# Fused attention, experts and dense layer: all weights through one ring of eight buffers, float64 pieces converted in place

## The chip, the cores and the metric

The kernel runs on one core of one Trainium2 chip. The metric is the device time of one execution in microseconds (us); lower is better. TensorE (PE) multiplies matrices, VectorE (DVE) and ScalarE (ACT) work on tiles in on-chip memory, GpSimd (POOL) and SyncE (SP) issue most of the DMA transfers here, and 16 DMA engines move the data.

## The reference

Three layers in a row on 1152 tokens: attention in a window of 64 positions, a mixture of eight experts of which each token goes to one, and a dense layer whose two weight matrices arrive as float64.

```
q, k, v: (2, 8, 576, 64) f32;   N, D, E, F = 1152, 512, 8, 1024
x = softmax(q k^T / 8, window of 64) v          -> (1152, 512)

expert_idx = argmax(x @ w_gate)                 # each expert takes at most 288 tokens
y = relu(x_e @ w1[e]) @ w2[e];  x = gate * y    # w1 (8,512,1024), w2 (8,1024,512) f32

h = x @ w_in                                    # w_in (512, 2048) float64
g = h * clip(h + 3, 0, 6) / 6
out = (g @ w_out).astype(float32)               # w_out (2048, 512) float64
```

## The kernel before

**Stages.** Attention and routing take the first 67 us or so. Then come 32 expert units and eight dense units. A unit is a quarter of an expert's weights (256 of 1024 inner columns) or an eighth of the dense layer's (256 of 2048): two halves, h = 0 for the up product and h = 1 for the down product, each 128 x 1024 float32 words. Expert units are called m0 to m31 here, dense units d0 to d7. They are worked off in three teams of experts and then in four groups of tokens of the dense layer:

```
ORDER = ('awwbawbwawbwabww', 'awwawwawwaww', 'awwbawbwaabwbwww')
GROUPS = [(0, 640, 0, NDS // 2), (640, 512, 0, NDS), (0, 384, NDS // 2, NDS), (384, 256, NDS // 2, NDS)]
```

A letter is one step of PE: `w` is half a unit of the team's large expert (208 to 256 tokens), `a` a unit of a smaller one, `b` a unit of a second small one, which in two teams is "tiny" (64 tokens). m0 to m11 belong to the first team; m2, the first `b`, is tiny. A dense step f uses unit f // 2: group 0 (640 tokens) takes d0 to d3 with eight steps, group 1 (512 tokens) all eight units. A step of the dense layer is called up(f) and down(f); PE does up(0), up(1), down(0), up(2), down(1) and so on.

**Weights.** Every product is made of three passes of rounded operands: hi x hi, lo x hi, hi x lo. So each loaded half is split in two pieces by `split_ops`: ACT casts hi (L263), and DVE subtracts for lo (L268), into one of eight `wt` buffers. Only a tiny unit is used by PE as loaded, and holds its `raw` buffers until then. Float64 has no hardware type: a "piece" is 128 x 512 float64 words, read as 128 x 1024 32-bit words, and `conv64` makes float32 of it in six steps: ACT abs (L207) and round (L210), DVE clamp (L214), shift (L218), join (L223) and add (L232). Four pieces are a dense unit.

**Buffers and queues.** `rawp` has six buffers of 4 KB in each partition for expert halves and for converted dense halves; `cv` has three `raw64` buffers of the same size for float64 pieces, and two of 2 KB each for `c64` and `t64`. SP issues the expert loads (L276, L279) and the float64 pieces of d2 to d7. GpSimd issues the gathers of tokens (L801), the eight pieces of d0 and d1 (L198, L201), which are converted while the experts run, stored to DRAM from `t64` (L235, `wd_dram`) and loaded again as float32 halves (L1130) ahead of the dense layer.

**Order.** The instructions of an engine run in the order in which the program writes them. A planner in the kernel's Python code makes this order: `add_job` gives each load, conversion and split a due time in units, and `advance` puts the first job in due order that fits into the estimated gaps of an engine. The ring objects (`r_raw`, `r_64`, `r_t`, `r_wt`) hold a job back until the planner's estimate has a buffer for it. In the dense layer each block of PE (`d_stage`) is followed by ACT r (L1554), DVE gf (L1557), ACT hi (L1560) and DVE g (L1563). The token matrix of the dense layer is x2, written by ACT and DVE at the end of each expert (L1384, L1386).

Of the kernel before, what the change touches and what calls it, by code (L numbers as in the profile page):

```python
# [9 lines left out]
F32 = mybir.dt.float32  # L10
# [13 lines left out]
def tile_kernel(ctx, tc, q, k, v, w_gate, w1, w2, w_in, w_out, out, cap):  # L24
# [152 lines left out]
    HW = UW // 4  # L177
    NSC = 2
    cv = ctx.enter_context(tc.tile_pool(name="cv", bufs=2))
    wd_dram = [dram.tile([128, UW], F32, name=f"wd_dram{u}") for u in range(NSC)]  # L180
    w_in32 = w_in.bitcast(U32)
# [3 lines left out]

    def conv64(u, i, dst):

        box = {}  # L190

        queue = nc.gpsimd if u < NSC else nc.sync

        def load():
            box["raw"] = raw = cv.tile([128, 2 * HW], U32, name="raw64", bufs=NR64)
            if i < 2:
                src = w_in32[256 * i : 256 * i + 256, 2 * FU * u : 2 * FU * u + 2 * FU]
                queue.dma_start(raw.rearrange("p (c f) -> p c f", c=2), src.rearrange("(c p) f -> p c f", p=128))  # L198
            else:
                r0 = FU * u + 128 * (i - 2)  # L200
                queue.dma_start(raw, w_out32[r0 : r0 + 128, :])  # L201
            w = raw.rearrange("p (n t) -> p n t", t=2)
            box["lo"], box["hi"] = w[:, :, 0], w[:, :, 1]

        def c_abs():
            box["c"] = cv.tile([128, HW], U32, name="c64", bufs=NC64)
            nc.scalar.activation(box["c"].bitcast(F32), box["hi"].bitcast(F32), AF.Abs)  # L207
# [29 lines left out]
        return load, c_abs, c_round, c_clamp, c_shift, a_join, t_add, store  # L237

    NR64, NC64, NT64 = 3, 2, 2

# [82 lines left out]
    with ExitStack() as actx:  # L323
# [482 lines left out]
        def early_gather(e):  # L806
            box["xE"] = t = cv.tile([128, HW], U32, name="c64", bufs=NC64).bitcast(F32)
            rows_of(t, eI[:, 1:2], 128 * NE)
# [29 lines left out]
        def early_relu(u):  # L838
            def run(e):
                if "hfE" not in box:  # L840
                    box["hfE"] = cv.tile([128, HW], F32, name="t64", bufs=NT64)
                    box["hE"] = cv.tile([128, HW], F32, name="t64", bufs=NT64)
# [29 lines left out]
        def early_out(e):  # L872
            box["yE"] = t = cv.tile([128, HW], U32, name="c64", bufs=NC64).bitcast(F32)
            copy(e, t, box["aE"])
# [86 lines left out]
        def first_gather(e):  # L961
            box["x0"] = t = cv.tile([128, HW], U32, name="c64", bufs=NC64).bitcast(F32)
            rows_of(t, sidx[:, 3 * RANKS[0] : 3 * RANKS[0] + 1])
# [57 lines left out]
    NWT = 4  # L1021
    NRAW = 3
    NPC = 4
# [46 lines left out]
    AHEAD = (3.0, 1.5)  # L1070
    ZDUE = 3

# [23 lines left out]

    r_raw, r_wt, r_64, r_ct, r_t = Ring(2 * NRAW), Ring(2 * NWT), Ring(NR64), Ring(NC64), Ring(NT64)

# [4 lines left out]

    wt_at, raw_at = {}, {}
    for m in range(len(units)):
# [4 lines left out]
    raw_t, raw_ready, wt, half_ready, stored, pieces = {}, {}, {}, {}, {}, {}  # L1110
    e_of = {}
# [6 lines left out]
    def load_job(m, h):  # L1118
        kind, s, u = units[m]

        def gate():
            if kind == "d" and stored.get((u, h), 0) < 2:
                return None
            return r_raw.free(raw_at[m, h])

        def run(e, fin):
            take_raw(m, h)
            t = raw_t[m, h]
            if kind == "d":
                nc.gpsimd.dma_start(t, wd_dram[u][:, HALF * h : HALF * h + HALF])  # L1130
            else:
                if u == 0:
                    e_of[s] = expert(s)
                x = e_of[s]
                weights_in(t, x, u, h)
# [7 lines left out]
    def conv_job(u, i, m=None):  # L1143
        h = i // 2
        ix = {}

        def dst():
            return None if m is None else raw_t[m, h][:, HW * (i % 2) : HW * (i % 2) + HW]

        load, c_abs, c_round, *mid, t_add, store = conv64(u, i, dst)  # L1150

        def gate_load():
            a = 0.0 if m is None or (m, h) in raw_t else r_raw.free(raw_at[m, h])
            b = r_64.free()
            return None if a is None or b is None else max(a - 2.0, b)

        def run_load(e, fin):
            if m is not None and (m, h) not in raw_t:
                take_raw(m, h)
            ix["raw"] = r_64.take()  # L1160
            load()
            return (fin if m is not None else spend("D", 1.46, fin)) + 2.0

# [12 lines left out]
        def run_add(e, fin):  # L1176
            if m is None:
                ix["t"] = r_t.take()
            t_add()
            r_64.rel[ix["raw"]] = r_ct.rel[ix["ct"]] = fin  # L1180
            if m is not None:
                raw_ready[m, i] = fin + 0.2
            return fin + 0.2

        def run_store(e, fin):
            store()
            r_t.rel[ix["t"]] = fin + 5.0
            stored[u, h] = stored.get((u, h), 0) + 1
            return fin

        now = lambda: 0.0
        ops = [({"D": 1.46} if m is not None else {"P": 1.1}, gate_load, run_load), ({"A": 0.6}, r_ct.free, run_abs)]
        ops.append(({"A": 0.57}, now, plain(c_round)))
        ops += [({"V": c}, now, plain(fn)) for c, fn in zip((0.34, 0.34, 0.61), mid)]
        ops.append(({"V": 0.61}, now if m is not None else r_t.free, run_add))
        return ops + ([({"P": 1.1}, now, run_store)] if m is None else [])

    def split_job(m, i):
# [8 lines left out]
        def run_high(e, fin):  # L1207
            if (m, h) not in wt:
                r_wt.take()
                wt[m, h] = wp.tile([128, 2, HALF], F32R, name="wt")  # L1210
            n = HALF // 2
            r = raw_t[m, h][:, n * (i % 2) : n * (i % 2) + n]
            high, box["low"] = split_ops(wt[m, h], r, i % 2)
            high(e)
            return fin + 0.2

        def run_low(e, fin):
            box["low"]()
            pieces[m, h] = pieces.get((m, h), []) + [fin]
            if len(pieces[m, h]) == 2:  # L1220
                r_raw.rel[raw_at[m, h]] = half_ready[m, h] = max(pieces[m, h])
            return fin
# [444 lines left out]
    def dense_again():  # L1667

        for t0 in range(0, NTOK, 512):
            n = min(512, NTOK - t0)  # L1670
            acc = [bank("acc") for _ in range(n // 128)]
            for u in range(DFF // FU):
                halves = [wk.tile([128, 2, NC, 256], F32R, name="xT256", bufs=XTB) for _ in range(2)]
                halves = [x.rearrange("p a c f -> p a (c f)") for x in halves]
                for i in range(NPC):
                    r = wk.tile([128, HW], F32, name="xg", bufs=3)
                    if u < NSC:
                        nc.sync.dma_start(r, wd_dram[u][:, HW * i : HW * i + HW])
                    else:
                        load, *mid, t_add, _ = conv64(u, i, lambda: r)  # L1680
                        for fn in (load, *mid, t_add):
                            fn()
                    high, low = split_ops(halves[i // 2], r, i % 2)
# [188 lines left out]
    est["D"] = max(est["D"], done["rk"] + 1.7)  # L1872
    for ring, t in ((r_64, est["P"]), (r_ct, done["g0"] + 4.0), (r_t, done["g0"] + 4.0)):
        ring.rel = [t] * ring.n
# [113 lines left out]
```

## Time and profile before

| | |
|---|---|
| median of three runs | 435.39 us (435.08 to 438.6) |
| the profiled execution's own time | 434.86 us |
| its span, first to last instruction | 432.9 us |
| granted TensorE clock, mean | 0.992 |
| PE busy | 406.1 us, 94% |
| DVE busy | 290.0 us, 67% |
| ACT busy | 241.4 us, 56% |
| DMA, mean over the span | 171 GB/s, 73.89 MB |

Busy shares are means over stages that differ; the tables by window and the rows of single engines below are read by stage. Start times are counted from the first instruction of the span. A step "start to start" is the difference of the start times of two neighbours in a timeline, since the listed durations of neighbours overlap.

### The profile page before, as it was taken

The page shows a single profiled execution, that of the slowest core. Times are in us where ns is not written, and L with a number is a line of the kernel's source. Part 1 is how long each engine was busy: PE and PEld are TensorE (multiplying, and loading weights), DVE is VectorE, ACT ScalarE, POOL GpSimd, SP SyncE. Part 2 cuts the span into 40 slices and gives each one's busy share as a digit, 9 for nine tenths or more (in the row PEclk, how much of TensorE's full clock was granted, in tenths as well). Part 3 has the DMA queues.
Part 4 walks back from the last instruction along what each step waited for, and adds up shares of the span by engine and source line. Part 5 has one row for each costly group of instructions (what it writes and reads, how often), then busy time and mean ns, then how long its engine had stood idle before and what let it go on. Part 6 is the DMA issues. An engine that isn't in the chain of part 4 may idle for free.

```text
span 432.9 us, 8533 instructions
## 1 busy us (share of the span) xinstructions
PE 406.1 (94%) x3055; PEld 345.4 (80%) x3055; DVE 290.0 (67%) x800; ACT 241.4 (56%) x527; POOL 62.5 (14%) x128
## 2 busy tenths in 40 slices
PE   7999888798899999999999999999999999999991
PEld 4887664597778989987899898888888888899981
DVE  2888967687789999717579999989843222323430
ACT  4886773584569887526587766577543222322320
POOL 8633405025022001000200000000000000200210
PEclk9999999999999999999999999999999999999996
DMA  9997857989999999656924465543100000100101
GB/s 172 203 232 179 273 216 233 363 288 372 364 313 372 287 344 286 198 180 216 385 91 135 117 172 162 150 142 105 44 0 0 2 0 2 60 37 2 49 30 51
DMA packets 67762, 73.89 MB, mean 171 GB/s; under 512 B 31008, under 2 KB 49440, under 8 KB 67712
## 3 DMA queue, kind: packets, MB, share of 16 engines
q1 hardware_dynamic: 63760, 59.79, 46.6%
q0 software_dynamic: 3952, 13.47, 8.4%
q8 instruction: 26, 0.43, 0.4%
q14 instruction: 24, 0.20, 0.1%
HBM read 66.44 MB, written 6.82 MB: 169 GB/s over the span
## 4 chain that ended last, share of the span: by engine, by line
PE 65%; DVE 14%; DMA 10%; ACT 5%; issue 3%; POOL 0%; POOLq 0%; ACTq 0%; DVEq 0%; SPq 0%
PE banks L249 52%; DVE wt L268 4%; DMA raw<-in_moe_w_dram 4%; PE banks L506 2%; DMA c<-x_dram,eI 2%; PE banks L624 2%; DMA c<-x_dram,sidx 1%; PE banks L1493 1%; PE banks L1468 1%; PE banks L570 1%; PE banks L606 1%; DVE c L223 1%; DVE g L1563 1%; PE banks L663 1%; ACT wt L263 1%
## 5 line engine op out<-in xcount | busy, mean ns | idle before, releaser
L249 PE MATMUL banks<-x,wt 128*128 128x320 f32 (+3 forms) x576 | 107.4, 337 | 1.8 <-DVE wt L268 1.4
L249 PEld LDWEIGHTS banks<-x,wt 128*128 128x128 f32 x576 | 94.3, 188 | 12.2 <-DVE wt L268 2.2
L268 DVE TENSOR_TENSOR wt<-raw,wt 128x512 fp32r<-128x512 f32 x128 | 82.8, 684 | 14.9 <-ACT wt L263 14.3
L249 PE MATMUL banks<-wt,g 128*128 128x512 f32 x384 | 92.8, 390 | 0.0
L263 ACT CAST wt<-raw 128x512 fp32r<-128x512 f32 x128 | 74.6, 620 | 15.8 <-DMA raw<-in_moe_w_dram 9.4
L249 PEld LDWEIGHTS banks<-wt,g 128*128 128x128 f32 x384 | 71.6, 188 | 14.2
L1557 DVE SCALAR_TENSOR_TENSOR gf<-r,banks 128x320 f32<-128x320 f32 (+3 forms) x48 | 26.5, 552 | 54.5 <-ACT r L1554 54.3
L1554 ACT ACTIVATE r<-banks,c_three 128x320 f32<-128x320 f32 (+3 forms) x48 | 27.8, 579 | 58.3 <-PE banks L249 58.1
L249 PE MATMUL banks<-xT,wt 128*128 128x256 f32 (+2 forms) x288 | 39.0, 284 | 0.5 <-DVE wt L268 0.3
L249 PEld LDWEIGHTS banks<-xT,wt 128*128 128x128 f32 x288 | 35.1, 191 | 2.7 <-DVE wt L268 0.8
L249 PE MATMUL banks<-h,wt 128*128 128x256 f32 (+2 forms) x288 | 37.0, 279 | 0.0
L249 PEld LDWEIGHTS banks<-h,wt 128*128 128x128 f32 x288 | 34.6, 191 | 0.5 <-issue 0.5
L1563 DVE TENSOR_TENSOR g<-gf,g 128x320 fp32r<-128x320 f32 (+2 forms) x40 | 23.4, 584 | 12.3 <-ACT g L1560 11.6
L207 ACT ACTIVATE c<-raw 128x512 f32<-128x512 f32 x32 | 21.7, 677 | 17.1 <-DVE raw L232 6.3
L1560 ACT CAST g<-gf 128x320 fp32r<-128x320 f32 (+2 forms) x40 | 21.3, 533 | 16.3 <-DVE gf L1557 16.2
L1600 POOL DMA_INDIRECT out_dram<-raw,cidx x4 | 4.0, 992 | 163.8 <-ACT raw L1597 156.2
L249 PE MATMUL banks<-wt,xT 128*128 128x256 f32 x144 | 22.1, 294 | 3.0 <-DVE wt L268 2.2
L249 PEld LDWEIGHTS banks<-wt,xT 128*128 128x128 f32 x144 | 18.7, 190 | 5.7 <-DVE wt L268 3.6
L596 ACT ACTIVATE pe<-neg,nmx 128x128 f32<-128x128 f32 x72 | 22.3, 392 | 0.1
L583 DVE CUSTOM_DVE_ANT_0 neg<-banks,tmask 128x128 f32<-128x128 f32 x72 | 16.2, 285 | 9.1 <-PE banks L570 9.1
L223 DVE SCALAR_TENSOR_TENSOR c<-raw,c 128x512 uint32<-128x512 uint32 x32 | 22.0, 686 | 0.4
L210 ACT ACTIVATE raw<-raw 128x512 uint32<-128x512 uint32 x32 | 21.6, 674 | 0.0
(287 smaller groups left out, 556.0 us busy)
## 6 DMA issues: line engine op xcount, KB each, us to landing
raw<-in_moe_w_dram SPq DMA_DIRECT2D x64, 512.0 KB, 6.0
raw<-in_moe_w_in_dram SPq DMA_DIRECT2D x12, 512.0 KB, 3.8
raw<-in_moe_w_out_dram SPq DMA_DIRECT2D x12, 512.0 KB, 3.7
early<-in_moe_w_dram SPq DMA_DIRECT2D x8, 512.0 KB, 7.3
x_dram<-xt SPq DMA_DIRECT2D x9, 256.0 KB, 2.9
q_sb<-in_q_dram SPq DMA_DIRECT2D x8, 256.0 KB, 4.8
k_sb<-in_k_dram SPq DMA_DIRECT2D x8, 256.0 KB, 4.8
v_sb<-in_v_dram SPq DMA_DIRECT2D x8, 256.0 KB, 4.7
```

Of the source, the lines that this page charges most:

```text
L207: nc.scalar.activation(box["c"].bitcast(F32), box["hi"].bitcast(F32), AF.Abs)
L210: nc.scalar.activation(box["lo"], box["lo"], AF.Copy, scale=2.0 ** -29)
L223: nc.vector.scalar_tensor_tensor(out=box["c"], in0=box["hi"], scalar=0xC0000000, in1=box["c"], op0=ALU.bitwise_and, op1=ALU.bitwise_or,)
L249: nc.tensor.matmul(out, l, r, start=(start and n == 0), stop=(stop and n == len(pairs) - 1))
L263: nc.scalar.copy(hi, r)
L268: V.tensor_tensor(out=lo, in0=r, in1=hi.bitcast(F32), op=ALU.subtract)
L583: V.tensor_tensor_reduce(out=neg[:, hp, :], in0=box["sp", g][:, hp, :], in1=tmask[:, first, :], scale=-1.0, scalar=3.0e38, op0=ALU.add, op ...
L596: nc.scalar.activation(pe[:, hp, :], neg[:, hp, :], AF.Exp, bias=nmx[:, hp : hp + 1], scale=-1.0)
L1554: nc.scalar.activation(r, ph, AF.Relu, bias=c_three)
L1557: V.scalar_tensor_tensor(out=gf, in0=r, scalar=6.0, in1=ph, op0=ALU.min, op1=ALU.mult)
L1560: nc.scalar.copy(hi, gf)
L1563: V.tensor_tensor(out=lo, in0=gf, in1=hi.bitcast(F32), op=ALU.subtract)
```

## The change

One ring of `NRAW` = 8 buffers (the six and, in size, two of the three `raw64`) takes every load of weights, and its positions are fixed ahead: `raw_at` counts expert halves and float64 pieces in the order of units, with the pieces of d0 put behind the units `FIRST_AT` = 5, 9, 14 and 20. All of them are issued by SP. A float64 piece takes a whole buffer and is converted where it lies: the add writes over the low words, 8 bytes apart, and the split reads it there. Only d0 is converted among the experts, into four tiles of 2 KB (`first_w`) that stay on chip until the dense layer; nothing is stored to DRAM and loaded again. d1 is now treated like d2 to d7, with a due time of 1.5 units ahead of its own. `first_w` also serves the two tiles of the early expert that had used `t64`.

```diff
-    NRAW = 3
+    NRAW = 8
+    FIRST_AT = (5, 9, 14, 20)
...
-    rawp = ctx.enter_context(tc.tile_pool(name="rawp", bufs=2 * NRAW))
+    rawp = ctx.enter_context(tc.tile_pool(name="rawp", bufs=NRAW))
...
         def load():
-            box["raw"] = raw = cv.tile([128, 2 * HW], U32, name="raw64", bufs=NR64)
+            box["raw"] = raw = rawp.tile([128, 2 * HW], F32, name="raw").bitcast(U32)
...
-                queue.dma_start(raw, w_out32[r0 : r0 + 128, :])
+                nc.sync.dma_start(raw, w_out32[r0 : r0 + 128, :])
...
         def t_add():
-            d = dst()
-            if d is None:
-                box["t"] = d = cv.tile([128, HW], F32, name="t64", bufs=NT64)
-            nc.vector.tensor_tensor(out=d.bitcast(U32), in0=box["c"], in1=box["lo"], op=ALU.add)
-
-        def store():
-            nc.gpsimd.dma_start(wd_dram[u][:, HW * i : HW * i + HW], box["t"])
+            out = box["lo"] if dst is None else dst.bitcast(U32)
+            nc.vector.tensor_tensor(out=out, in0=box["c"], in1=box["lo"], op=ALU.add)
...
+    first_w = [cv.tile([128, HW], F32, name=f"first_w{i}", bufs=1) for i in range(4)]
...
     for m in range(len(units)):
+        if m != dense0:
+            for n in range(2 if units[m][0] == "e" else NPC):
+                raw_at[m, n] = len(raw_at)
+            for i in range(NPC):
+                if FIRST_AT[i] == m:
+                    raw_at[dense0, i] = len(raw_at)
         for h in range(2):
-            raw_at[m, h] = len(raw_at)
...
-            if kind == "d" and u >= NSC:
-                add_job(m - AHEAD[1] + 0.1 * i, m, conv_job(u, i, m))
+            if m == dense0:
+                add_job(FIRST_AT[i] + 1, FIRST_AT[i], conv_job(m, i))
             elif kind == "d":
-                add_job(m + ZDUE + 0.1 * i, m, conv_job(u, i))
-        if kind == "e" or u < NSC:
+                add_job(m - AHEAD[1] + 0.1 * i, m, conv_job(m, i))
+        if kind == "e":
```

PE's order of instructions is the same in both kernels. GpSimd's queue in the first expert team, the kernel before (`xg` is a gather of tokens, `raw64` a float64 piece, `t64` a converted one):

```order
L801 DMA xg_1512<-x_dram_78,sidx_130 64x512
L198 DMA raw64_1552<-in_moe2_w_in_dram 128x2x512
L198 DMA raw64_1554<-in_moe2_w_in_dram 128x2x512
L201 DMA raw64_1568<-in_moe2_w_out_dram 128x1024
L235 DMA wd_dram0_101<-t64_1666 128x512
L201 DMA raw64_1708<-in_moe2_w_out_dram 128x1024
L801 DMA xg_1785<-x_dram_78,sidx_130 128x512
L235 DMA wd_dram0_101<-t64_1781 128x512
L198 DMA raw64_1826<-in_moe2_w_in_dram 128x2x512
L801 DMA xg_1831<-x_dram_78,sidx_130 128x512
```

The same place on GpSimd's queue in the changed kernel:

```order
L791 DMA xg_1512<-x_dram_78,sidx_132 64x512
L791 DMA xg_1764<-x_dram_78,sidx_132 128x512
L791 DMA xg_1802<-x_dram_78,sidx_132 128x512
L791 DMA xg_1825<-x_dram_78,sidx_132 96x512
L791 DMA xg_2291<-x_dram_78,sidx_132 128x512
```

Only the gathers are left; the pieces of d0 stand in SP's queue, the first of them between the second half of m5 and the first half of m6.

DVE around the last writes of x2 ahead of the dense layer, the kernel before (`wt_3429` and `wt_3454` are the two halves of d0, `c64_3533` belongs to the first piece of d2):

```order
L268 TENSOR_TENSOR wt_3429<-raw_3347,wt_3429 128x512 x2
L1364 SCALAR_TENSOR_TENSOR h_3432<-banks_82,h_3432 128x208
L1344 TENSOR_LOAD offI_1458
L1412 ISA
L1412 TENSOR_TENSOR x2_1616<-banks_82,x2_1616 128x4x64
L268 TENSOR_TENSOR wt_3454<-raw_3349,wt_3454 128x512
...
L1386 TENSOR_TENSOR x2_1616<-banks_82,x2_1616 128x2x208
L1386 ISA
L1386 TENSOR_TENSOR x2_1616<-banks_82,x2_1616 128x2x208
L214 TENSOR_SCALAR c64_3533<-c64_3533 128x512
```

The same place in the changed kernel (`first_w0` and `first_w1` are the first half of d0, `c64_3392` and `c64_3461` belong to the third and fourth piece of d1):

```order
L1363 ISA
L1363 TENSOR_TENSOR x2_1616<-banks_82,x2_1616 128x2x208
L1363 ISA
L1363 TENSOR_TENSOR x2_1616<-banks_82,x2_1616 128x2x208
L258 TENSOR_TENSOR wt_3439<-first_w0_101,wt_3439 128x512
L258 TENSOR_TENSOR wt_3439<-first_w1_102,wt_3439 128x512
L217 SCALAR_TENSOR_TENSOR c64_3392<-raw_3302,c64_3392 128x512
L224 ISA raw_3302<-raw_3302,c64_3392 128x512x2
L208 TENSOR_SCALAR c64_3461<-c64_3461 128x512
L212 TENSOR_SCALAR c64_3461<-c64_3461 128x512
L217 SCALAR_TENSOR_TENSOR c64_3461<-raw_3304,c64_3461 128x512
L1534 SCALAR_TENSOR_TENSOR gf_3503<-r6_3502,banks_82 128x320
```

The splits of d0 have moved from ahead of the last writes of x2 to behind them, and conversions of d1 stand there where those of d2 stood.

## Rows read from the trace of the kernel before

**Rows 1.** The page, part 1: busy us (share of the span) xinstructions.

```profile
PE 406.1 (94%) x3055; PEld 345.4 (80%) x3055; DVE 290.0 (67%) x800; ACT 241.4 (56%) x527; POOL 62.5 (14%) x128
```

**Rows 2.** The chain of waits, longest pieces: start us, us, what.

```profile
100.60 12.88 DMA raw<-in_moe_w_dram
...
264.15 159.71 PE banks L249 x783
```

**Rows 3.** Windows: us, busy (x) of PE, PEld, DVE, ACT, POOL, PEclk, DMA share, GB/s.

```profile
110.00:120.00 10.00, 8.82 (x71) 7.39 (x68) 7.63 (x25) 6.38 (x14) 0.78 (x2) 1.00 1.06 374
...
210.00:220.00 10.00, 10.00 (x87) 8.70 (x85) 6.30 (x12) 6.56 (x15) 1.54 (x3) 1.00 0.92 359
...
240.00:250.00 10.00, 9.10 (x51) 7.89 (x50) 9.70 (x20) 6.50 (x13) 0.00 (x0) 1.00 0.51 146
```

**Rows 4.** PE, timeline, first expert team: start us, us, instruction [idle before <-releaser].

```profile
106.28 0.71 PE L249 MATMUL banks<-wt,xT 128*128 128x256 f32 x4
...
115.69 1.09 PE L1468 MATMUL banks<-raw,xT 128*64 128x128 f32 x16 [1.08 <-DMA raw<-in_moe_w_dram]
116.71 1.66 PE L249 MATMUL banks<-wt,h 128*128 128x512 f32 x6
118.20 1.60 PE L249 MATMUL banks<-xT,wt 128*128 128x256 f32 x12
119.64 1.60 PE L249 MATMUL banks<-h,wt 128*128 128x256 f32 x12
...
124.51 1.08 PE L1493 MATMUL banks<-raw,h 128*64 128x256 f32 x8
```

**Rows 5.** DMA issues: line, engine, count, KB each, us to landing.

```profile
raw<-in_moe_w_in_dram POOLq DMA_DIRECT2D x4, 512.0 KB, 8.7
...
wd_dram<-t POOLq DMA_DIRECT2D x8, 256.0 KB, 6.0
```

**Rows 6.** POOL, timeline: the seventh store.

```profile
126.41 0.55 POOL L235 DMA_DIRECT2D wd_dram<-t  x1 [4.30 <-DVE t L232]
```

**Rows 7.** SP, timeline: loads of expert weights, the eleventh.

```profile
93.54 0.37 SPq L276 DMA_DIRECT2D raw<-in_moe_w_dram  x1
```

**Rows 8.** DVE, timeline, first expert team.

```profile
105.83 0.69 DVE L232 CUSTOM_DVE_ANT_0 t<-raw,c 128x1024 uint16<-128x1024 uint16 x1 [2.87 <-DMA wd_dram<-t]
```

**Rows 9.** PE, timeline, second and third team.

```profile
139.88 0.93 PE L249 MATMUL banks<-xT,wt 128*128 128x224 f32 x6 [0.29 <-DVE wt L268]
...
195.31 0.48 PE L249 MATMUL banks<-wt,xT 128*128 128x256 f32 x2
196.43 1.70 PE L249 MATMUL banks<-wt,xT 128*128 128x256 f32 x10 [0.64 <-ACT wt L263]
```

**Rows 10.** DVE, timeline, start of the dense layer.

```profile
223.12 0.59 DVE L1386 TENSOR_TENSOR x<-banks,x 128x416 f32 x1 [0.33 <-ACT x L1384]
...
225.47 0.49 DVE L1557 SCALAR_TENSOR_TENSOR gf<-r,banks 128x320 f32<-128x320 f32 x1 [0.90 <-ACT r L1554]
...
263.41 0.69 DVE L268 TENSOR_TENSOR wt<-raw,wt 128x512 fp32r<-128x512 f32 x1
```

**Rows 11.** DVE, timeline, start of the dense layer, neighbours in a row.

```profile
227.78 0.42 DVE L218 TENSOR_SCALAR c<-c 128x512 uint32<-128x512 uint32 x1
228.12 0.69 DVE L232 CUSTOM_DVE_ANT_0 raw<-raw,c 128x1024 uint16<-128x1024 uint16 x1
228.72 0.49 DVE L1563 TENSOR_TENSOR g<-gf,g 128x320 fp32r<-128x320 f32 x1
229.12 0.48 DVE L1557 SCALAR_TENSOR_TENSOR gf<-r,banks 128x320 f32<-128x320 f32 x1
229.52 0.68 DVE L223 SCALAR_TENSOR_TENSOR c<-raw,c 128x512 uint32<-128x512 uint32 x1
```

**Rows 12.** DVE by line: duration ns min/median/max, first and last start us.

```profile
L232 DVE CUSTOM_DVE_ANT_0 raw<-raw,c x24: 680/686/695, 228.1 to 311.3; 128x1024 uint16<-128x1024 uint16 x24
...
L268 DVE TENSOR_TENSOR wt<-raw,wt x128: 675/683/694, 72.3 to 328.4; 128x512 fp32r<-128x512 f32 x128
```

More of the change, by code (lines that the diff above doesn't have):

```diff
@@ L177, in tile_kernel @@
     HW = UW // 4
-    NSC = 2
     cv = ctx.enter_context(tc.tile_pool(name="cv", bufs=2))
-    wd_dram = [dram.tile([128, UW], F32, name=f"wd_dram{u}") for u in range(NSC)]
     w_in32 = w_in.bitcast(U32)
@@ L205, in c_abs @@
         def c_abs():
-            box["c"] = cv.tile([128, HW], U32, name="c64", bufs=NC64)
+            box["c"] = cv.tile([128, HW], U32, name="c64")
             nc.scalar.activation(box["c"].bitcast(F32), box["hi"].bitcast(F32), AF.Abs)
@@ L228, in t_add @@
         def t_add():
[L229 to L239 removed]
+            out = box["lo"] if dst is None else dst.bitcast(U32)
+            nc.vector.tensor_tensor(out=out, in0=box["c"], in1=box["lo"], op=ALU.add)
+        return box, (load, c_abs, c_round, c_clamp, c_shift, a_join, t_add)
+    NC64 = 2
+    first_w = [cv.tile([128, HW], F32, name=f"first_w{i}", bufs=1) for i in range(4)]
     NFU = F // FU
@@ L806, in early_gather @@
         def early_gather(e):
-            box["xE"] = t = cv.tile([128, HW], U32, name="c64", bufs=NC64).bitcast(F32)
+            box["xE"] = t = cv.tile([128, HW], U32, name="c64").bitcast(F32)
             rows_of(t, eI[:, 1:2], 128 * NE)
@@ L840, in run @@
                 if "hfE" not in box:
-                    box["hfE"] = cv.tile([128, HW], F32, name="t64", bufs=NT64)
-                    box["hE"] = cv.tile([128, HW], F32, name="t64", bufs=NT64)
+                    box["hfE"] = first_w[0]
+                    box["hE"] = first_w[1]
                 if e == "A":
@@ L872, in early_out @@
         def early_out(e):
-            box["yE"] = t = cv.tile([128, HW], U32, name="c64", bufs=NC64).bitcast(F32)
+            box["yE"] = t = cv.tile([128, HW], U32, name="c64").bitcast(F32)
             copy(e, t, box["aE"])
@@ L961, in first_gather @@
         def first_gather(e):
-            box["x0"] = t = cv.tile([128, HW], U32, name="c64", bufs=NC64).bitcast(F32)
+            box["x0"] = t = cv.tile([128, HW], U32, name="c64").bitcast(F32)
             rows_of(t, sidx[:, 3 * RANKS[0] : 3 * RANKS[0] + 1])
@@ L1095, in take @@
             return len(self.rel) - 1
-    r_raw, r_wt, r_64, r_ct, r_t = Ring(2 * NRAW), Ring(2 * NWT), Ring(NR64), Ring(NC64), Ring(NT64)
+    r_raw, r_wt, r_ct = Ring(NRAW), Ring(2 * NWT), Ring(NC64)
     def whole(m):
@@ L1104, in tile_kernel @@
     wt_at, raw_at = {}, {}
+    dense0 = unit_of["d", 0, 0]
     for m in range(len(units)):
+        if m != dense0:
[4 more added lines that the diff above has]
+                    raw_at[dense0, i] = len(raw_at)
         for h in range(2):
-            raw_at[m, h] = len(raw_at)
             if not whole(m):
                 wt_at[m, h] = len(wt_at)
-    raw_t, raw_ready, wt, half_ready, stored, pieces = {}, {}, {}, {}, {}, {}
+    raw_t, raw_ready, wt, half_ready, pieces = {}, {}, {}, {}, {}
     e_of = {}
@@ L1118, in load_job @@
     def load_job(m, h):
-        kind, s, u = units[m]
+        _, s, u = units[m]
         def gate():
-            if kind == "d" and stored.get((u, h), 0) < 2:
-                return None
             return r_raw.free(raw_at[m, h])
@@ L1127, in run @@
             take_raw(m, h)
[L1128 to L1135, printed above, removed]
+            if u == 0:
+                e_of[s] = expert(s)
+            weights_in(raw_t[m, h], e_of[s], u, h)
             raw_ready[m, 2 * h] = raw_ready[m, 2 * h + 1] = fin + 2.0
@@ L1141, in load_job, with conv_job @@
         return [({"D": 1.46}, gate, run)]
-    def conv_job(u, i, m=None):
-        h = i // 2
+    def conv_job(m, i):
+        u = units[m][2]
         ix = {}
[L1147 to L1155, printed above, removed]
+        first = m == dense0
+        b, (load, c_abs, c_round, *mid, t_add) = conv64(u, i, first_w[i] if first else None)
         def run_load(e, fin):
-            if m is not None and (m, h) not in raw_t:
-                take_raw(m, h)
-            ix["raw"] = r_64.take()
+            r_raw.take()
             load()
-            return (fin if m is not None else spend("D", 1.46, fin)) + 2.0
+            raw_t[m, i] = first_w[i] if first else b["lo"].bitcast(F32)
+            return fin + 2.0
         def run_abs(e, fin):
@@ L1176, in run_add @@
         def run_add(e, fin):
-            if m is None:
-                ix["t"] = r_t.take()
             t_add()
-            r_64.rel[ix["raw"]] = r_ct.rel[ix["ct"]] = fin
-            if m is not None:
-                raw_ready[m, i] = fin + 0.2
+            r_ct.rel[ix["ct"]] = fin
+            if first:
+                r_raw.rel[raw_at[m, i]] = fin
+            raw_ready[m, i] = fin + 0.2
             return fin + 0.2
[L1185 to L1189, printed above, removed]
         now = lambda: 0.0
-        ops = [({"D": 1.46} if m is not None else {"P": 1.1}, gate_load, run_load), ({"A": 0.6}, r_ct.free, run_abs)]
+        ops = [({"D": 1.46}, lambda: r_raw.free(raw_at[m, i]), run_load), ({"A": 0.6}, r_ct.free, run_abs)]
         ops.append(({"A": 0.57}, now, plain(c_round)))
         ops += [({"V": c}, now, plain(fn)) for c, fn in zip((0.34, 0.34, 0.61), mid)]
-        ops.append(({"V": 0.61}, now if m is not None else r_t.free, run_add))
-        return ops + ([({"P": 1.1}, now, run_store)] if m is None else [])
+        ops.append(({"V": 0.61}, now, run_add))
+        return ops
     def split_job(m, i):
@@ L1211, in run_high @@
             n = HALF // 2
-            r = raw_t[m, h][:, n * (i % 2) : n * (i % 2) + n]
+            r = raw_t[m, h][:, n * (i % 2) : n * (i % 2) + n] if units[m][0] == "e" else raw_t[m, i]
             high, box["low"] = split_ops(wt[m, h], r, i % 2)
@@ L1219, in run_low @@
             pieces[m, h] = pieces.get((m, h), []) + [fin]
+            if units[m][0] == "d" and m != dense0:
+                r_raw.rel[raw_at[m, i]] = fin
             if len(pieces[m, h]) == 2:
-                r_raw.rel[raw_at[m, h]] = half_ready[m, h] = max(pieces[m, h])
+                half_ready[m, h] = max(pieces[m, h])
+                if units[m][0] == "e":
+                    r_raw.rel[raw_at[m, h]] = half_ready[m, h]
             return fin
@@ L1675, in dense_again @@
                 for i in range(NPC):
[L1676 to L1682, printed above, removed]
+                    b, ops = conv64(u, i)
+                    for fn in ops:
+                        fn()
+                    r = b["lo"].bitcast(F32)
                     high, low = split_ops(halves[i // 2], r, i % 2)
@@ L1872, in tile_kernel @@
     est["D"] = max(est["D"], done["rk"] + 1.7)
-    for ring, t in ((r_64, est["P"]), (r_ct, done["g0"] + 4.0), (r_t, done["g0"] + 4.0)):
+    for ring, t in ((r_ct, done["g0"] + 4.0),):
         ring.rel = [t] * ring.n
```

6 lines of the change are left out of this document (2 added, 4 removed).

## Prediction

> **What bounds the kernel now.** I read the page's first part first: TensorE is busy for 94% of the span [rows 1]. Some 27 us are not PE's, and a good part of those lies in the attention and routing stages ahead of 67 us, which the diff does not touch. The chain of waits then says where the rest is: one piece of 12.88 us hangs on a load of expert weights in flight from 100.60 to 113.48, and from 264.15 on the chain is PE alone to the end [rows 2]. So there are two stretches in which this change can move the end: the first expert team (about 85 to 125 us) and the start of the dense layer (222 to 264 us). What it does later must first spoil a stretch in which PE never waits.
>
> In the first stretch the windows show the 16 DMA engines full (share 1.06 at 374 GB/s) while PE is busy 8.82 of 10 us [rows 3]: loads end last there. PE's own row of blocks gives the size. From 106.28 to 124.51 PE takes 18.2 us. The blocks issued in that time are six of 12 matmuls, each 1.44 undisturbed (118.20 to 119.64), two tiny blocks of 1.02 (115.69 to 116.71), one of six wide ones at 1.49 (116.71 to 118.20) and small transposes of about 0.2: 12.4 us [rows 4]. **5.8 us are lost** in 18; the one wait of PE in brackets there, 1.08 us, names the load itself.
>
> In the second stretch DMA is at half share and DVE is busy 9.70 of 10 us, while PE drops to 9.10 [rows 3]. There VectorE ends last: it converts float64 pieces and splits them, beside two operations for each block of the dense layer.
>
> **The change in the expert stretch.** GpSimd's queue loses eight loads of 512 KB, eight stores of 256 KB and four reloads of 512 KB [rows 5]; SP's queue gains eight loads, four of which (first dense unit) stay among the experts and four (second unit) go behind them. By 126.41 us, when its seventh store was issued, GpSimd had taken all eight loads, 6.0 MB in all [rows 6]; now two loads, 1 MB, belong to that stretch. The 5 MB less are, at the 374 GB/s of the window, 13 us of full DMA engines. On SP's queue m5.0, the eleventh load, was issued only at 93.54 [rows 7], because its buffer of six was held by the tiny unit m2 until PE had used it. With eight buffers that wait falls on the thirteenth load (the first dense piece) and m6.0 behind it: m5.0 and m5.1 go out with the early ones, while all that stands behind that point starts a buffer or two ahead of before. Both together should remove the load wait.
>
> VectorE has a part in it: at 105.83 the add of a conversion waited 2.87 us because its output buffer was still being stored to DRAM, and behind it in order stood the h of an expert step and the splits for which PE then waited [rows 8]. The store is gone, and so is that wait. Three or more conversions leave the stretch as well. What is late next is the split on ACT and DVE, so I don't take the whole: **5.2 of the 5.8 us** (ends: 2, if the split or the queue keeps PE, and 5.8).
>
> Later stalls are of the same kind. From 195.31 two matmuls of a block of 12 take 1.12 us, where 0.24 is their share of 1.44: 0.9 us lost to a cast on ACT that came late [rows 9]. In the new order of VectorE the splits of that unit stand ahead of an expert step's h and not behind it; I take the **0.9**. At 139.88 a half block waits 0.29 us for a split [rows 9], and two like it follow by 162, 0.9 us at that size; VectorE starts this stretch with less arrears; I take **0.7**. Sum here: 5.2 + 0.9 + 0.7 = 6.8 us.
>
> **The change at the dense start.** The second unit's four conversions used to be done among the experts; now they fall around the last writes of x2, and the first unit's four splits, which stood ahead of these writes, stand behind them. The part before the writes is hidden: about 3.5 us of conversion in a stretch where VectorE is busy 6.30 of 10 us [rows 3]. The part behind is not. PE's step up(6) was resumed at 264.15, right when the split that began at 263.41 had ended [rows 2, 10]: the row of DVE work from the last x2 write (223.12) to that split sets this time. I counted it in the order of both kernels. Before: 12 clamps, 11 shifts, 11 joins, 10 adds, 10 splits, 12 gf and 12 g; now 12, 12, 13, 12, 14, 12 and 12. Start to start, a shift takes 0.34, an add 0.60, g 0.40, gf 0.40 [rows 11]; a join (0.68 listed) and a split (683 ns) are listed as long as an add (686 ns) [rows 11, 12] and counted like one, a clamp like a shift (12 in both kernels). That is 36.1 us before and 41.2 now, **5.1 more**. Measured, the row took 40.4 us (223.71 to 264.10), so 4.3 us of it were waits.
>
> If every wait stays, PE is 5.1 us later, and 5.7 if waits grow with the row (40.4 / 36.1). If the new work fills all 4.3 us, it is 0.9. The one wait that I can place, 0.90 us at 225.47 until the first block's r is there [rows 10], is filled, since the first unit's splits and a join stand there now; with the shorter waits of this kind for later blocks I take 1.4 us as filled: **3.7 us lost**, nearer the upper end because the rest look like waits between dependent operations of one conversion, of which there are more now. Behind group 0 nothing more is added: units 4 to 7 are needed only halfway through group 1, and ACT, which gets two operations for each conversion moved here, is busy 6.50 of 10 us [rows 3]. The DRAM reloads that had to be in by 222 us are gone, which costs and gives nothing by itself, as PE did not wait for them.
>
> **In-place adds.** The add (L232) now writes where it reads, words 8 bytes apart, in place of a dense tile. In the profile it is a custom operation on 1024 16-bit elements and takes 686 ns, as long as a split of 512 words [rows 12], so it handles two halves a step; it already reads the float64 words with gaps at this speed. No row shows it write with gaps. By the nearest rows it is between nothing and one half a step: g of 320 takes 0.40 and the add's 512 steps 0.60, some 1.04 ns a step, so 512 more steps are 0.53 us for each add. I take nothing, as the gapped read is the nearest row. The Trainium skill (VectorE: DVE Perf Modes, section "What auto-detection actually checks") says that an operation with two sources gets two results a cycle where every tensor is 16-bit with step plus or minus one; read strictly, pairs with gaps between them would lose it, and the adds would cost the 0.53; this case's gapped reads at full speed speak for the milder reading. Freeing the dense float32 tiles costs nothing.
>
> **Sum.** 434.86 − 6.8 + 3.7 = 431.8 us against the profiled execution's own time, which is 0.5 us below the median of the three runs, well inside their scatter.
>
> **Rivals.**
> 1. *The pinch at the dense start is filled.* Waits absorb most of the 5.1 us, some 1.4 are left: 434.86 − 6.8 + 1.4 = 429.5. For it: 4.3 us of waits are there, and VectorE is idle over a third of the time just before. Against: PE already waited in this stretch, twice.
> 2. *The stalls among experts stay.* One queue now carries everything in a fixed order. The first dense piece stands behind m5.1 and waits for the tiny unit's buffer, which was free only at 93.54 [rows 7], and all later expert loads stand behind it. If they come no earlier, PE gains only the store's wait and some bandwidth, about 2 us: 434.86 − 2 + 3.7 = 436.6. Against: DMA was full then, and 5 MB leave.
> 3. *The other side: gapped adds at one half a step.* Ten to twelve adds stand in the row that releases up(6); ten at 0.53 make 5.3 us, and 434.86 − 6.8 + 3.7 + 5.3 = 437.1, slower than before. It decides from (6.8 − 3.7) / 10 = 0.31 us an add.
> 4. *Nothing moves*: PE's waits are replaced one for one, 434.9.
>
> **How the numbers follow.** A measurement of this kernel tells about 1% (4.4 us) from no change. Forecast 431.8: 0.43; rival 1: 0.27; rival 2: 0.14; rival 3: 0.10; rival 4: 0.06. Faster by over 1% means below 430.5: nearly all of rival 1 and a third of the forecast's own spread (430 to 434), 0.41. Slower by over 1% means above 439.2: the ends of rivals 2 and 3 with the 5.7 us pinch, 0.09. The rest is 0.50. The range goes from rival 1 with a pinch of 0.9 and the whole 7.6 gained (428.2) and half a us for small waits of the same kind, 427.5, to rivals 2 and 3, 437.5.
>
> **What would show it.** Right: no GpSimd load or store between 74 and 130 us, DMA share below 1 from 90 to 125 us, PE from 106.28's block to 124.51's within 13 us, the dense start some 7 us sooner, DVE without a gap from there, group 0 longer by 3 to 4 us with PE waiting for L258 splits. Wrong: PE's stalls at loads before 125 us, adds longer than 0.69 us, or a stall of PE behind group 0.

## The result and the profile after

The changed kernel took 430.06 us (median of four runs, 428.94 to 432.31) beside 435.24 us for the kernel before: ratio 0.9893, 95% interval 0.9849 to 0.9938. A later set of runs gave 0.9901 (0.9871 to 0.9931). That is 5.2 us faster, where 431.8 had been forecast.

Four start times in PE's timeline split the span into stretches, here for two profiles of each kernel. "m1" is the first block of unit m1 (the first `banks<-wt,xT` block of 12), "dense" the first block of the dense layer, "group 1" its first block of 512 columns.

| profile | m1 | dense | group 1 | span | m1 to dense | group 0 | group 1 to end |
|---|---|---|---|---|---|---|---|
| before | 84.99 | 222.21 | 277.26 | 432.9 | 137.22 | 55.05 | 155.64 |
| before, second (`b_again`) | 87.25 | 223.57 | 278.27 | 433.9 | 136.32 | 54.70 | 155.63 |
| after | 87.78 | 217.45 | 275.96 | 430.6 | 129.67 | 58.51 | 154.64 |
| after, second (`a_again`) | 87.29 | 217.05 | 275.53 | 429.9 | 129.76 | 58.48 | 154.37 |

The experts gained 7.5 us from first profile to first, group 0 lost 3.5, the end gained 1.0, and the start of m1 moved by 2.8; the second profile of the kernel before moved by 2.3 without any change. By the second profiles the three are 6.6, 3.8 and 1.3. The dense start came 4.8 us sooner, and not the 7 that the prediction named, since m1 began later; counted from m1 it is the 7.5.

PE's timeline of the changed kernel in the first expert team, to be read against [rows 4]: no block has a wait in brackets, and from the first half block of `banks<-wt,xT` (109.13, answering to 106.28) to the tiny block (122.19, answering to 124.51) it takes 13.1 us, where it was 18.2.

```profile
109.13 1.67 PE L239 MATMUL banks<-wt,xT 128*128 128x256 f32 x12
...
122.19 1.08 PE L1470 MATMUL banks<-raw,h 128*64 128x256 f32 x8
```

The windows of the same kernel (busy us of PE, PEld, DVE, ACT, POOL, clock, DMA share, GB/s) answer to [rows 3]: PE is full, and the DMA engines have room.

```profile
100.00:110.00 10.00, 10.00 (x85) 8.74 (x84) 6.32 (x17) 5.30 (x13) 0.00 (x0) 1.00 0.70 237
110.00:120.00 10.00, 10.00 (x83) 8.63 (x82) 7.94 (x25) 6.42 (x15) 0.00 (x0) 1.00 0.90 283
```

The kernel before had two waits for a split (L268) in group 0, besides one of 0.36 us for x2 at its start:

```profile
248.90 3.51 PE L249 MATMUL banks<-x,wt 128*128 128x320 f32 x20 [0.86 <-DVE wt L268]
...
264.15 2.90 PE L249 MATMUL banks<-x,wt 128*128 128x320 f32 x18 [0.50 <-DVE wt L268]
```

The changed kernel has four, all for a split (L258):

```profile
219.29 7.03 PE L239 MATMUL banks<-x,wt 128*128 128x320 f32 x44 [0.67 <-DVE wt L258]
...
231.51 3.50 PE L239 MATMUL banks<-x,wt 128*128 128x320 f32 x20 [1.19 <-DVE wt L258]
...
246.92 3.51 PE L239 MATMUL banks<-x,wt 128*128 128x320 f32 x20 [0.96 <-DVE wt L258]
...
262.26 3.50 PE L239 MATMUL banks<-x,wt 128*128 128x320 f32 x20 [0.88 <-DVE wt L258]
```

The last of them ends with the first of two splits that stand at 261.52 in DVE's timeline (ended at about 262.21): the splits for up(6), which the prediction had named.

The rows of the add by line (ns min/median/max) show the gapped writes (`raw`) beside dense ones (`first_w`), to be read against [rows 12]:

```profile
L224 DVE CUSTOM_DVE_ANT_0 raw<-raw,c x28: 682/686/695, 211.4 to 322.5; 128x1024 uint16<-128x1024 uint16 x28
...
L224 DVE CUSTOM_DVE_ANT_0 first_w<-raw,c x4: 681/688/694, 103.3 to 168.6; 128x1024 uint16<-128x1024 uint16 x4
```

686 ns with gaps and 688 without: converting in place costs nothing. The strict reading of the Trainium skill (VectorE: DVE Perf Modes, section "What auto-detection actually checks"), by which pairs with gaps would lose the double rate, doesn't hold for these pairs; the measurement decides.

### The profile page after: what moved, and what is told of

Its sections match the earlier page's. It is cut to its first block, busy times and chain, and to the rows that moved or that the text cites. A ratio compares the mean times of both kernels' runs of the same rounds, so it can differ in the third digit from the quotient of the medians.

```text
span 430.6 us, 8492 instructions
## 1 busy us (share of the span) xinstructions
PE 405.8 (94%) x3055; PEld 345.2 (80%) x3055; DVE 290.8 (68%) x801; ACT 241.8 (56%) x526; POOL 50.7 (12%) x108
## 4 chain that ended last, share of the span: by engine, by line
PE 71%; DVE 14%; DMA 5%; ACT 4%; issue 4%; POOL 0%; POOLq 0%; ACTq 0%; DVEq 0%
PE banks L239 57%; DVE wt L258 5%; PE banks L496 2%; PE banks L1470 2%; PE banks L1445 2%; DMA c<-x_dram,eI 2%; DMA c<-x_dram,sidx 2%; PE banks L614 1%; PE banks L560 1%; DVE c L217 1%; PE banks L596 1%; PE banks L1281 1%; DVE raw L224 1%; PE banks L653 1%; DMA raw<-in_moe_w_in_dram 1%
## 5 line engine op out<-in xcount | busy, mean ns | idle before, releaser
L239 PE MATMUL banks<-x,wt 128*128 128x320 f32 (+3 forms) x576 | 108.7, 338 | 3.9 <-DVE wt L258 3.7
L258 DVE TENSOR_TENSOR wt<-raw,wt 128x512 fp32r<-128x512 f32 x124 | 80.8, 687 | 16.1 <-ACT wt L253 15.8
L253 ACT CAST wt<-raw 128x512 fp32r<-128x512 f32 x124 | 73.3, 630 | 11.3 <-PE banks L239 6.4
L791 POOL DMA_INDIRECT xg<-x_dram,sidx x10 | 12.8, 1275 | 81.4 <-PE banks L1281 66.2
L239 PE MATMUL banks<-wt,xT 128*128 128x256 f32 x144 | 20.1, 289 | 0.0
```

The lines of the kernel that those rows point to most:

```text
L239: nc.tensor.matmul(out, l, r, start=(start and n == 0), stop=(stop and n == len(pairs) - 1))
L253: nc.scalar.copy(hi, r)
L258: V.tensor_tensor(out=lo, in0=r, in1=hi.bitcast(F32), op=ALU.subtract)
```

## The experiments

The theory was: the experts gain because 5 MB of transfers leave full DMA engines, and group 0 loses because the second unit's conversions lengthen the row of VectorE work ahead of the splits that PE needs. Rivals were the deeper ring for the first, and the gapped adds or the displaced splits of d0 for the second. Every ratio below is to runs of the kernel before that were taken beside it.

**The same kernels again.**

`a_again` is the changed kernel without an edit.

> The changed kernel once more, to see whether its early stall belongs to it. In its first profile PE waited 2.81 us at 81.95 us (1.55 in the kernel before) and was granted a clock of 0.83 in the window from 80 to 90 us; its four runs lie between 428.9 and 432.3 us. Theory: the stall belongs to the kernel (the ring of eight lets SP issue the eighth to tenth load 1 to 3 us earlier, and the half of m1 that PE needs lands 1.4 us later), so it is there again, with 2.5 us or more of wait, and the time is 429 to 432. Rival: it varies from run to run, and then a profile of a run near 429 shows 1.5 us or less there and a clock of 1.00.

430.11 us (428.84 to 431.72). The profile (of a run of 431.7 us) shows PE waiting 2.30 us at 81.09 and a clock of 0.83 from 80 to 90 us. That alone would have spoken for the theory of the expectation, that the early stall belongs to the change.

`b_again` is the kernel before without an edit, profiled once.

> The kernel before once more, for a second profile of its early stretch. In its first profile the half of m1 that PE needs was cast at 78.05 us and the first block of m1 began at 84.99; in the changed kernel at 87.78 and 87.29. If the later start belongs to the change, this profile shows 85 to 86 again with a clock of 1.00 from 80 to 90 us; if it varies from run to run, it may show 87 to 88 and a clock of 0.83. Experts (first block of m1 to first dense block) 137, group 0 55 us.

435.82 us. PE's timeline and the window of that profile:

```profile
81.21 1.08 PE L1304 MATMUL banks<-ident,xg 128*128 128x128 f32 x4 [3.00 <-issue]
82.08 3.01 PE L249 MATMUL banks<-early,t 128*128 128x512 f32 x4
...
85.83 1.98 PE L249 MATMUL banks<-early,t 128*128 128x512 f32 x4
```

```profile
80.00:90.00 10.00, 8.71 (x38) 5.62 (x38) 4.63 (x10) 4.88 (x11) 0.00 (x0) 0.83 1.04 369
```

The kernel before has the same stall, with 3.00 us, where its first profile had 1.55. The theory falls: the start of m1 varies, between 84.28 and 88.13 over all the profiles of this study, in either kernel, and says nothing about the change.

**What holds the experts: bytes or buffers.**

`a_traffic` adds transfers that nobody reads to the changed kernel, on GpSimd's queue behind four gathers:

```diff
...
+    SPARE = {3: 3, 4: 2, 5: 2, 6: 3}
...
+        for _ in range(SPARE.get(len(gathers), 0)):
+            n = len(spare)
+            spare.append(n)
+            nc.gpsimd.dma_start(spare_dram[n], w_out32[128 * n : 128 * n + 128, :])
```

> The changed kernel with ten further copies of 512 KB from DRAM to DRAM on GpSimd's queue, issued behind the third to sixth gather of tokens (about 75 to 105 us); nothing reads them. They bring back some 5 MB of the transfers that the change took out, without stores for which an engine waits. If the bytes were what held the loads, PE stalls come back between 85 and 125 us, 3 to 6 us of them, and the time is 433 to 436. If the store wait of VectorE and the six buffers were the cause, PE stays without a stall there and the time within 1 us of the changed kernel.

441.96 us (438.45 to 444.99), ratio 1.0204 (1.0146 to 1.0263): more than forecast. In the profile (438.45 us, the fastest of the four runs) m1 to dense took 137.20 us, as in the kernel before. The chain of waits (start us, us, what) shows loads again:

```profile
72.89 17.36 DMA raw<-in_moe_w_dram
...
92.65 13.84 DMA raw<-in_moe_w_in_dram
```

When the first of these two loads had landed (72.89 + 17.36 = 90.25), ScalarE cast it at 90.27, after 5.15 us of waiting, and the copy that PE needed stood behind that cast. PE's wait, and the window:

```profile
91.43 1.11 PE L1387 MATMUL banks<-ident,c 128*128 128x128 f32 x4 [3.45 <-ACT c L453]
```

```profile
90.00:100.00 10.00, 8.10 (x42) 6.83 (x42) 6.18 (x14) 6.82 (x15) 2.46 (x4) 0.66 1.07 393
```

With two smaller waits (0.47 and 0.84 us) PE waited 4.8 us between 85 and 125 us, which is inside the expected 3 to 6. Much of the rest is the clock: behind the long wait the window shows 0.66, part of it at the lower of the two levels (1.2 and 2.4 GHz), and the block of 12 begun at 93.09 is listed with 2.93 us, where the same block has 1.70 in the changed kernel. So the bytes alone are enough to take back the 7.5 us, by waits and by the clock that follows them. They sit earlier than the old ones did, so PE stalls from 86 us on and not from 106. The other three runs took up to 6.5 us longer than the profiled one; why is open.

`b_nsc1` takes away half of the extra bytes in the kernel before, and with them four of the eight early conversions and stores, and leaves its buffers:

```diff
-    NSC = 2
+    NSC = 1
```

> The kernel before with only the first dense unit taken through DRAM: four loads, four stores and two reloads on GpSimd's queue instead of eight, eight and four; the second unit is loaded by SP and converted at the dense start, into the six buffers, through the three float64 buffers. It takes half of the extra bytes (2.6 of 5 MB) from the first expert team and keeps ring and queues. If bytes are what holds the experts, the stretch from the first block of m1 to the first dense block goes from 137.2 about halfway to 129.7: 133 to 134 us. If the ring makes the gain, it stays at 136 or more. Group 0 gets the second unit's conversions as in the changed kernel: 58 to 60 us. Time 434 to 437.

440.81 us (439.39 to 441.59), ratio 1.0119 (1.0073 to 1.0164); m1 to dense 134.14 us, group 0 63.12. Half of the bytes give 3.1 of the 7.5 us (2.2 of 6.6 against the second profile of the kernel before), with the old ring: the first part came nearly as forecast. The wait of VectorE for a store is still there, 3.00 us at 108.36, so this part isn't its doing. The windows from 100 to 120 us of the kernel before and of this one:

```profile
100.00:120.00 20.00, 17.47 (x138) 14.47 (x135) 14.72 (x43) 10.34 (x24) 5.83 (x9) 1.00 1.05 370
```

```profile
100.00:120.00 20.00, 18.52 (x140) 15.03 (x139) 14.02 (x41) 9.15 (x22) 3.90 (x5) 0.91 1.00 338
```

Group 0 was the miss, 3 us longer than the expectation's upper end. Counted in its order, the row of VectorE work from the last x2 write to up(6)'s split is some 43 us there, about 6.8 more than before, and group 0 became 8.1 longer. Some 1.5 us of group 0 are the clock: behind waits of 2.17 and 1.13 us the block of 20 begun at 236.79 took 4.87 us to the next block, where the one begun at 255.91 took 3.35, and the windows from 235 to 245 us show 0.79 and 0.87.

`a_ring6` and `a_ring7` take buffers from the changed kernel:

```diff
-    NRAW = 8
+    NRAW = 6
```

> The changed kernel with six ring buffers in place of eight. If the gain among the experts comes from the bytes that GpSimd no longer moves and from the store that VectorE no longer waits for, the stretch from the first block of m1 to the first dense block stays near 129.7 us (137.2 in the kernel before) and the time within 2 us of the changed kernel. If it comes from the deeper ring, that stretch goes back towards 135 us or more and the time to 434 or more. The early stall goes back to about 1.5 us if the earlier issue of loads makes it. At the dense start fewer pieces can lie ready, which may cost some us more in group 0.

> The changed kernel with seven ring buffers. With six, PE lost 14.6 us more among the experts, at a DMA share of 0.53, so SP waited for buffers there and not for the DMA engines. If eight leaves room, seven costs 0 to 3 us among the experts (129.7 to 133 us from the first block of m1 to the first dense block). If every buffer counts alike, seven costs some 7 us (137 us, about the kernel before). Group 0 stays at 58 to 60 us; the time is 430 to 438.

With six 445.4 us (ratio 1.0251, 1.0214 to 1.0288), with seven 434.92 (0.999, 0.9959 to 1.002). m1 to dense: 144.30 us with six, 133.98 with seven, 129.67 with eight; group 0 59.01, 58.74, 58.51. A window, SP's timeline and the longest wait of SP there (us in total, times, longest) with six:

```profile
110.00:120.00 10.00, 7.08 (x31) 5.31 (x32) 7.78 (x14) 4.55 (x10) 0.00 (x0) 0.66 0.53 164
```

```profile
105.19 0.37 SPq L269 DMA_DIRECT2D raw<-in_moe_w_dram  x1
113.63 0.37 SPq L266 DMA_DIRECT2D raw<-in_moe_w_dram  x1
```

```profile
SPq L266 <- DVE first_w L224: 7.9, 1, 7.9
```

PE is held up here with half of the DMA engines idle: for 8.4 us SP issued nothing, since the next load's buffer was not free. The wait names what held it: the first float64 piece of d0, which lay in its buffer until the last step of its conversion, the add at 112.82. With eight buffers that add stands at 103.33. So a piece that waits for its conversion holds up the loads of experts behind it. The clock has a part in the 10 us too: the window shows 0.66, and the block of 12 begun at 117.66 took 2.48 us, the next one 1.44. (The early stall was 2.91 us with six buffers, so it doesn't come from the earlier issue of loads either.)

Bytes held the kernel before, and the buffers would hold the changed one if it had fewer. At equal bytes the ring of eight does no better than the old six and three: 137.20 us in `a_traffic`, 137.22 in the kernel before. So the gain looks like that of the bytes, and eight buffers only take back what the float64 pieces cost in the common ring; but the copies of `a_traffic` lie at other times than the old transfers, and the kernel before with a deeper ring and all its bytes, which would settle it, was not run.

The expectation for seven was met in neither of its forms among the experts; the first lost buffer costs 4.3 us and the second 10.3. In group 0, six and seven buffers have one long wait each (3.33 and 3.07 us) and then a block of 14 of 4.90 us, where 3.31 is usual, so 1.6 us of their 59.01 and 58.74 are the clock (0.66 in the five us around it).

**What makes group 0 longer.**

`a_two_early` converts d1 among the experts as well, with eight `first_w` tiles and six ring buffers:

```diff
-    first_w = [cv.tile([128, HW], F32, name=f"first_w{i}", bufs=1) for i in range(4)]
+    first_w = [cv.tile([128, HW], F32, name=f"first_w{i}", bufs=1) for i in range(8)]
...
-    NRAW = 8
-    FIRST_AT = (5, 9, 14, 20)
+    NRAW = 6
+    FIRST_AT = (5, 7, 9, 11, 14, 17, 20, 23)
...
```

> The changed kernel with the second dense unit treated like the first: its four pieces too are converted among the experts into tiles that stay on chip (behind units 5, 7, 9, 11, 14, 17, 20 and 23), and the ring has six buffers to make room. If the second unit's conversions are what makes group 0 longer, group 0 goes from 58.5 us back to 55 us or less (first dense block to first block of group 1), and the experts lose little: 426 to 429 us. If group 0 is long for another reason (adds that write with gaps, splits of the first unit behind the writes of x2), it stays at 57 us or more. Against the kernel with six buffers and one early unit the difference is that of the four conversions alone.

442.71 us (ratio 1.019, 1.0154 to 1.0226): the total was far off, because the experts took 147.46 us. `a_ring6` explains 144.30 of it by the six buffers; the other 3.2 came with four more pieces in the ring and were not followed up. Group 0 went from 59.01 us with six buffers to 54.09, 4.9 less. The count had 5.1, but the nearness is in part luck: 1.6 of the 4.9 are the block at the lower clock in `a_ring6`, and none is at it here. That the second unit's conversions lengthen group 0 is shown; without that block they are worth 3.3 us.

`a_d0_split_first` puts only the splits of d0 back ahead of the writes of x2:

```diff
-                add_job(m + 0.1 * i, m, split_job(m, i))
+                add_job(m + 0.1 * i - (1.0 if m == dense0 else 0.0), m, split_job(m, i))
```

> The changed kernel with the splits of the first dense unit due one unit sooner, so that they stand ahead of the last writes of x2 as in the kernel before; all else as it is. The first wait of PE in group 0 (0.67 us at 219.29, for the split of the first unit) goes away. If these four splits are a part of what makes group 0 longer, it becomes 57 to 57.5 us; if the wait for the later splits only grows by as much, it stays at 58.5. Time 429 to 430.

430.18 us (ratio 0.9899, 0.9851 to 0.9946), group 0 58.91 us. The first wait for a split is gone, up(2)'s is down to 0.39 us, up(6)'s is gone too, and two others are new or longer:

```profile
238.42 3.48 PE L239 MATMUL banks<-wt,g 128*128 128x512 f32 x14 [0.77 <-DVE wt L258]
...
244.30 4.87 PE L239 MATMUL banks<-x,wt 128*128 128x320 f32 x20 [1.83 <-DVE wt L258]
```

```profile
240.00:250.00 10.00, 8.17 (x38) 7.12 (x37) 9.41 (x19) 5.97 (x12) 0.00 (x0) 0.83 0.61 200
```

The time is that of the changed kernel. But behind the wait of 1.83 us the clock was lower, 0.83 in this window: the block of 20 begun at 244.30 took 4.71 us to the next block (249.01), where 3.35 is usual. Without these 1.4 us group 0 would be about 57.5, the upper end of the other branch of the expectation. So by themselves the four splits change nothing in the time, and whether they have a share of up to 1 us that the clock ate up stays open.

`a_ahead08` leaves everything and lets each conversion be due later, by which the splits of d0 also come to stand ahead of the last writes of x2:

```diff
-    AHEAD = (3.0, 1.5)
+    AHEAD = (3.0, 0.8)
```

> The changed kernel with one constant altered: a dense unit's conversion is due 0.8 units ahead of its own and not 1.5. In the order of VectorE the four splits of the first dense unit then stand ahead of the last writes of x2, and conversions of later units stand behind the splits that PE waits for: from the last x2 write to the split that up(6) waits for there are 35.7 us of operations, counted as in the prediction (41.2 in the changed kernel, 36.1 in the kernel before). If the row of VectorE work sets group 0, it goes from 58.5 to 55 us and the time to 426 to 428 us, without anything else being changed. Rival: the sum of conversions that must be done by then (twelve pieces, not eight) is what costs, wherever they stand; then group 0 stays at 58 us and the time at 430.

423.33 us (422.34 to 425.39), ratio 0.9736 (0.9699 to 0.9772): the fastest kernel of the study, and faster than its forecast. Experts 129.78 us, group 0 52.85. PE's timeline in group 0 has no wait at all; here is up(6), where the others waited:

```profile
252.91 3.79 PE L239 MATMUL banks<-x,wt 128*128 128x320 f32 x24
```

VectorE is as busy as ever (9.79 of 10 us from 240 to 250). What had cost time was not the amount of work but its order. By the count of the expectation 5.5 us less stand in front of up(6)'s split: 2.4 are the splits of d0, which by themselves had changed nothing in the time, and the rest are, on balance, conversions that PE doesn't need yet and that now stand behind it.

`b_ahead08` has the same edit in the kernel before.

> The kernel before with the due time of a dense unit's conversion at 0.8 units ahead and not 1.5, the constant that brought the changed kernel from 430 to 423 us. If that gain is one of order alone, independent of the ring, group 0 goes from 55 to 53 us here too and the time to 433; the experts stay at 137. If it needs the ring of eight, where pieces lie loaded and wait, this kernel's three float64 buffers make the conversions late, and group 0 becomes longer than 55 us.

433.51 us (431.44 to 434.79), ratio 0.995 (0.9914 to 0.9985). Group 0 52.84 us, experts 136.76: the order alone gives the old kernel its 2.2 us in group 0, and the ring isn't needed for it. Of the time 1.2 us are left (434.73 us for the kernel before beside it).

## Why the prediction was right

- *Experts, 5.2 us in the first team*: measured 5.2 (18.2 to 13.1 us, from the same block to the same block). The cause as named, bytes, is borne out from both sides: adding them takes the gain back, and halving them in the old kernel gives 3.1 of 7.5 with the store's wait still there. The ring's share is argued from runs at equal bytes, and not tested in the kernel before. The wait for a store [rows 8] is gone with the stores; its own share of the 5.2 wasn't isolated.
- *Later stalls, 0.9 and 0.7*: the block behind the cast took 1.12 + 1.63 us before; in the changed kernel the block at 191.93 took 1.61 in one piece, and none of the three stalls of about half a us between 138 and 162 is left. Both terms were sized small: start to start they gave some 1.1 and 1.4 us, less 0.6 for a new stall at 165.46 that waits for the scaled tokens (xg). All stretches of the experts together gave 7.5 us (6.6 by the second profiles) where 6.8 was forecast.
- *Dense start, 3.7 us*: measured 3.5 (3.4 to 3.8 over the pairs of profiles). Counting the operations in front of one split was the right tool here. From the last write of x2 to the split that released up(6) the row took 43.6 us (218.64 to 262.21), where it had been 40.4; the work in it is 40.6 us, one split less than the 41.2 counted, so 3.0 us are waits, 1.4 fewer than before, which is what the prediction took. (At the steps listed the row before comes to 36.0 us and the lower end to 0.8, not 36.1 and 0.9; nothing hangs on it.) Two of its parts were not right: the splits of d0 moved behind x2 cost the time nothing on their own, and the work in front of the split was taken as given, though by the same steps 5.0 us of it are conversions for d4 and 3.8 more are for the second half of d3, which up(6) doesn't use.
- *In-place adds at no cost*: right, and rival 3 falls with 686 ns.
- *Rival 2, the fixed order of one queue*: it didn't happen, but it was nearer than its chance said. With one buffer fewer the time is the old one, with two it is 11 us above it.
- *Rival 1, waits fill the pinch*: no; DVE's early wait was filled and PE still waited four times.
- *Not foreseen*: the end of the span is 1.0 us shorter. 7.5 − 3.5 + 1.0 = 5.0 by the first profiles and 4.0 by the second, beside 5.2 between the medians. The start of m1, which the prediction did not count on, varies by 4 us from run to run and is no part of it.

The sum came out 1.7 us above the measured median. By the first profiles that is the experts' extra 0.7 and the end's 1.0; by the second the experts gave 0.2 less than forecast and the end 1.3. So which term was off is known only to within the spread of the profiles, about 1 us.

## What to carry to other kernels

Where the DMA engines are full, look first for bytes that needn't move: a store and reload of an intermediate costs its bytes twice, and here the bytes of one queue held up the loads of the other. A common ring in a fixed order is worth what its depth allows, so try one buffer fewer, see whether the queue stops with the DMA engines half idle, and ask what holds the buffer that it waits for. On an engine that is busy nearly all the time and works in order, ask of each operation ahead of the one that is waited for whether anyone needs it yet; in the changed kernel a single due time gave 6.8 us, more than the whole change, and in the kernel before 1.2. And where a wait is priced by an experiment, look at the granted clock behind it: several stretches here hold 1.4 to 1.6 us of one slower block beside the wait itself.

## What the runs showed that was not expected

From the first block of group 1 to the end of the span the kernels with GpSimd loads and stores of weights took 155.3 to 155.7 us (155.0 with the spare copies), those without 154.2 to 154.8. PE's part of it is equal (277.26 to 423.85, and 275.96 to 422.54), so the difference lies behind the last matmul; most of it lies even behind GpSimd's last issue for the output (ended at 425.83, and at 424.53), from where 7.1 and 6.1 us are left. Its cause was not tried and stays open.

In the profiles in which PE waited 2 to 3 us near 81 us, the clock of that window was mostly 0.83 (one at 2.32 us kept 1.00): part of it at the lower level. In `b_again` the four wide matmuls begun at 82.08 took 2.85 us to the next block, the four begun at 85.83 took 1.42.
